# Moving a bank, a clip, one feed-forward item and several loads in the order of an attention kernel with a feed-forward block

## The chip, the cores and the metric

One Trainium2 chip, one of its cores. The metric is the device time of one execution in microseconds (us). The kernel is a single launch; everything below runs inside it.

## The reference

Two computations follow each other. The first is attention that is routed by clusters: each query and each key goes to the nearest of 16 centroids of its head, and a query attends only to the keys of its own cluster. The second takes the result as a matrix of 3072 tokens by 512 and runs a feed-forward block with a hard-swish gate.

```python
batch, n_heads, seq, head_dim = (4, 8, 768, 64)      # n_clusters = 16
q_assign = argmax(einsum('bhsd,hcd->bhsc', q_n, c_n), axis=-1)      # k_assign likewise
mask = q_assign[:, :, :, None] == k_assign[:, :, None, :]
scores = where(mask, scale * (q @ k^T), -1e9)
x = softmax(scores) @ v                              # then (B,H,S,D) -> (3072, 512)
h = x @ w_in                                         # 512 -> 2048
g = h * clip(h + 3.0, 0.0, 6.0) / 6.0
out = g @ w_out                                      # 2048 -> 512
```

## The kernel before, in words

The heads are taken in pairs: 16 pairs (`NPAIR`), four to a batch. The kernel has two stages and then a tail.

**First stage, pairs 0 to 7 (a loop over double steps `n`, two key blocks each).** Scores are full: `scores` puts them into `psum_s` (two buffers of two banks), `exponentials` reads them on ScalarE, `attn_v` multiplies by the values, `sum_up` adds up the denominators on TensorE (`pd`), and one step later VectorE takes the reciprocal and multiplies (lines 473 and 474). Into the same loop go the preparation of the next pair (`turn`, `cluster_scores`, `route`, `route_turn`), the decoding of the weights in small steps (`share` says how many), and the first items of the feed-forward block: `up_at` lists the double steps at which one item of two halves (`begin`, `end`) is taken from the list `fill`. `route` reads its tile `pr` on VectorE and writes `one_hot` (line 357); `route_turn` transposes `one_hot` on TensorE in two parts (line 379).

**Second stage, pairs 8 to 15 (`late_plan`, from `FIRST` on).** `whole.close()` gives back the memory of the first stage, the four score banks among it, and `open_late` opens new pools: `psum_y` with two banks and `psum_s` with one buffer of two. Here the rows of a pair are sorted by cluster so that scores need only a band. `order` and `positions` work out the place of each row (VectorE, lines 1000, 1009 and 1011). `scatter` (GpSimd) writes 24 pieces of rows, `qd` and `kvd`, to device memory by those places, out of the tiles `qn` and `kvn`, which `load_queries` and `load_keys` fill and of which there is one buffer each. `load_ranked` reads the sorted rows back: parts 0 and 1 into the tile `piece` (line 884), part 2 into `vs` (line 907). `turn_ranked` transposes a `piece` on TensorE (line 913), then come the band scores. After that `gather` fetches the results by the same places.

The order of the second stage is written by hand. `steps_of` gives each step of a pair an offset in points; there are 28 points to a pair (`SLOT`). At each point first the steps of the plan are emitted, in the order of the pairs and of the list, and then one half item of `fill`, except at two points of each pair. Each engine, and the queue of SyncE (SP) that issues nearly all loads and stores, then runs what it was given strictly in that order: a load that has to wait holds up every load behind it on SP.

**The feed-forward items.** A block is 256 tokens: `ffn_items` gives eight up items and seven down items per block. For the first block the up product is plain (`ph`, line 607): ScalarE lifts it (line 499), VectorE clips it (line 502), and after each odd item `gated_sums` forms four sums of the gate `g_sb` (line 645). For the other blocks the up product runs in halves with seven products for eight (`uX`, `uY`, line 655), which needs sums of weights in the tile `tx`; `first_sums` loads `tx` for the item after the next one from device memory (line 548, three buffers). In those blocks lift and clip are put off into the lists `lifting` and `ending`, which `raise_gates` and `finish` empty. The down items multiply `g_sb` by `w_out_sb` and by its sums `T1` to `T4` into two banks, `X` and `Y` (line 694). In the tiles named `m` of `psum_m` there are two banks, shared by turns between `ph`, `X`, `uX` and, in the first stage, the short tiles of the preparation (`pr`, `po`, `pd`, `pcs`, `pqk`).

**The tail.** What is left in `fill` runs with nothing beside it.

Of the kernel before, what the change touches and what calls it, by code (L numbers as in the profile page):

```python
# [8 lines left out]
F32 = mybir.dt.float32  # L9
# [9 lines left out]
P = 128  # L19
# [6 lines left out]
DM = 512  # L26
# [93 lines left out]
def fast_path(ctx, tc, ok, q, k, v, centroids, moe_w_in, moe_w_out, out):  # L120
# [3 lines left out]
    nc = tc.nc  # L124
# [53 lines left out]
    st = {}  # L178
# [322 lines left out]
    def clip(g, r, h):  # L501
        nc.vector.scalar_tensor_tensor(out=g, in0=r, scalar=1.0, in1=h, op0=ALU.min, op1=ALU.mult)  # L502
# [83 lines left out]
    def ffn_items(b):  # L586
        def up(m, i):
            u = (b * NHC + m) * HF + i
            g = g_sb[:, 0:4, i]
            got = {}  # L590

            def begin():
                raise_gates()
                load_block()
                if u >= HF:
                    first_sums(u + 2)
                    halved(b, m, u, i, got)

            def end():
                if u < HF:  # L600
                    for other in sooner.get(u, ()):
                        kept_sums(other)
                    ph = psum_m.tile([P, 512], F32, name="ph", tag="m")
                    for t in range(2):
                        f = t * HF + i
                        for kt in range(NKT):
                            nc.tensor.matmul(
                                ph[:, t * HC : (t + 1) * HC], lhsT=w_in_sb[:, kt, f * P : (f + 1) * P],
                                rhs=st["xb", b, m][:, kt], start=(kt == 0), stop=(kt == NKT - 1),
                            )  # L610
                    ph = ph.rearrange("p (k c) -> p k c", k=4)
                    lift(g, ph)
                    clip(g, g, ph)
                    gated_sums(i)
                else:
                    got["rest"](g)
                if i == HF - 1:
                    st.pop(("xb", b, m)), st.pop(("xs", b, m), None)
                    st["free"] = True
                    load_block()  # L620

            return [begin, end]
# [10 lines left out]
                op()  # L633
            ending.clear()

        def gated_sums(i):
            if i % 2 == 0:
                return
            a11, a21, a12, a22, s1, s2, s4 = (g_sb[:, k, i - 1 : i + 1] for k in range(7))
            eng = nc.vector if st["moving"] or (i == HF - 1 and st["last"]) else nc.gpsimd  # L640
            for out_, in0, in1, op in (
                (s1, a21, a22, ALU.add), (s2, s1, a11, ALU.subtract),
                (a21, a11, a21, ALU.subtract), (s4, a12, s2, ALU.subtract),
            ):
                eng.tensor_tensor(out=out_, in0=in0, in1=in1, op=op)  # L645
# [57 lines left out]
        def down(m, part):  # L703
            def keep(chunk, half, y, queue=nc.sync):
                queue.dma_start(out_v[b, 2 * m + chunk][:, half * HC : (half + 1) * HC], y)

            def multiply(second):
                if part < 2:
                    h = range(part * HF // 2, (part + 1) * HF // 2)
                    if second:  # L710
                        product(st["X"], 1, 5, st["T2"], False, True, False, h)
                    else:
                        product(st["X"], 0, 0, wb[0][0], True, False, False, h)
                    return
                kind, bank, half, w = (
                    (4, "Y", 0, st["T1"]), (1, "Y", 1, st["T3"]),
                    (2, "X", 0, wb[1][0]), (6, "Y", 0, wb[1][1]), (3, "Y", 1, st["T4"]),
                )[part - 2]
                h = range(second * HF // 2, (second + 1) * HF // 2)
                product(st[bank], half, kind, w, part == 2, part in (3, 4, 6), part > 3, h)  # L720

            def begin():
                raise_gates()
                if part == 0:
                    st["X"] = psum_m.tile([P, DM], F32, name="X", tag="m")
                    st["y0"] = yp.tile([P, DM], F32, name="y0", tag="y0")
                elif part == 2:
                    st["Y"] = st.get("psum_y", psum_m).tile([P, DM], F32, name="Y", tag="m")
                    st["y1"] = yp.tile([P, DM], F32, name="y1", tag="y1")
                multiply(0)  # L730

            def end():
                multiply(1)
                if part == 0:
                    finish()
                if (b, m, part) == (B - 1, NHC - 1, 6):
                    st["good"] = nc.values_load(ok[0:1, 0:1], min_val=0, max_val=1)
                if part == 4:
                    token_sums(*divmod(b * NHC + m + 1, NHC))
                y0, y1 = st["y0"], st.get("y1")  # L740
                if part == 1:
                    nc.scalar.copy(out=y0[:, HC:], in_=st["X"][:, HC:])
                    add(y0[:, HC:], y0[:, HC:], st["X"][:, 0:HC])
                elif part == 3:
                    add(y1[:, 0:HC], y0[:, HC:], st["Y"][:, HC:])
                    add(y1[:, HC:], y1[:, 0:HC], st["Y"][:, 0:HC])
                    keep(1, 1, y1[:, HC:])
                elif part == 4:
                    nc.scalar.copy(out=y0[:, 0:HC], in_=st["X"][:, 0:HC])
                    keep(0, 0, y0[:, 0:HC])  # L750
                elif part == 6:
                    add(y1[:, 0:HC], y0[:, HC:], st["Y"][:, HC:])
                    keep(1, 0, y1[:, 0:HC])
                    add(y0[:, HC:], y0[:, HC:], st["Y"][:, 0:HC])

                    keep(0, 1, y0[:, HC:], nc.scalar if st["last"] else nc.sync)
                if (b, m) == (0, 0):
                    for i in ([HF - 1, HF - 2], [5], [4], [], [3, 2], [0], [1])[part]:
                        make_first_sums(i)
                    if part in (0, 1):  # L760
                        weight_sums(6 + part)
                    elif part in (2, 3):
                        weight_sums(2 + part)

            return [begin, end]
# [420 lines left out]
    def steps_of(g):  # L1186

        first, last = g == FIRST, g == NPAIR - 1
        if first:
            plan = [  # L1190
                (-38, load_queries), (-37, load_keys, 0), (-36, load_keys, 1), (-37, run_up),
                (-36, step_up), (-31, order), (-30, positions), (-20, lambda g: st.pop("signed")()),
            ]
        else:
            plan = [
                (-46, load_natural, 0), (-45, load_natural, 1), (-38, turn_natural, 0), (-37, turn_natural, 1),
                (-36, cluster_scores), (-34, own_clusters), (-33, run_up), (-32, step_up), (-31, load_queries),
                (-29, order), (-28, positions), (-29, load_keys, 0), (-27, load_keys, 1),
            ]
        plan += [  # L1200
            (-29 if first else -24, scatter, 0), (-29 if first else -24, scatter, 1), (-12, band_masks), (-3, load_ranked, 0), (-3, load_ranked, 1),
            (-2, load_ranked, 2), (-1, turn_ranked, 0), (0, turn_ranked, 1),
        ]
        d = 1 if last else 2
        plan += [
            (d, band_scores, (0, 5), 1), (d + 2, band_scores, (2,), 3), (d + 4, band_scores, (4,)),
            (d + 4, band_values, 0), (d + 4, key_adds, 0, 1, 2), (d + 5, key_adds, 0, 3), (d + 7, band_values, 1),
            (d + 7, key_adds, 1, 1, 2), (d + 8, key_adds, 1, 3), (d + 10, band_sums),
            (12 if last else 14, band_divide), (14 if last else 16, keep_ranked),
            (15 if last else 23, gather), (28 if last else 37, turn_back),  # L1210
        ]
        return [(g, *step) for step in plan]
# [37 lines left out]
    decode += [lambda i=i: weight_sums(i) for i in range(4)]  # L1250
    st["kept"] = set()
    sooner = {0: (7,), 1: (6,), 2: (5,), 5: (4, 3)}
    up_at = (60, 64, 70, 72, 80, 84, 90, 94, 100)
    READY, DECODED = per_batch + 2 * lag_d, 2 * per_batch

    def share(n, r):
# [22 lines left out]
    with tc.manual_schedule():  # L1279
# [58 lines left out]
        st["early"] = False  # L1338
        st["moving"] = True
        open_late()  # L1340
        for i, point in enumerate(late_plan()):
            for op, *args in point:
                op(*args)
            busy = i >= AHEAD and (i - AHEAD) % SLOT in (6, 9)
            if fill and not busy:
                fill.pop(0)()
# [370 lines left out]
```

## Time and profile before

| | before |
|---|---|
| median of 3 runs | 954.39 us (954.17 to 955.42) |
| the profiled execution: its own time | 955.15 us |
| its span, first to last instruction | 953.4 us |
| granted TensorE clock, mean | 0.995 |
| TensorE busy (PE) | 930.6 us, 98% of the span |
| VectorE (DVE) | 595.6 us, 62% |
| ScalarE (ACT) | 349.7 us, 37% |
| GpSimd (POOL) | 574.6 us, 60% |
| HBM traffic | 129 GB/s over the span |

PE is TensorE's matmuls, DVE VectorE, ACT ScalarE, POOL GpSimd, SP SyncE, which is here only a queue of loads and stores. A row of a timeline reads: start in us from the span's start, duration (of the whole group if several are merged, with xcount), engine, line of the kernel, operation, tile written <- tiles read, shape, and in brackets the idle time of the engine before it and what ended it.

### The profile page before, as it was taken

What the parts mean: (1) busy time and instruction counts of PE and PEld (TensorE: products, weight loads), DVE (VectorE), ACT (ScalarE), POOL (GpSimd) and SP (SyncE); (2) the same over time, 40 slices, a digit from 0 to 9 for tenths busy, and PEclk for the clock granted to TensorE, in tenths of its full rate; (3) what the DMA queues carried; (4) which work ended last, traced back from release to release, by engine and by line L of the source; (5) the groups of instructions that cost most, each with busy time, mean ns of one, the idle gap of its engine ahead of it and who ended that gap; (6) DMA issues with size and microseconds to landing.
All of it is one profiled execution on the core that took longest, in us unless ns stands there. A gap on an engine that the chain in (4) does not pass through costs nothing.

```text
span 953.4 us, 17615 instructions
## 1 busy us (share of the span) xinstructions
PE 930.6 (98%) x6358; PEld 728.2 (76%) x6358; DVE 595.6 (62%) x1306; ACT 349.7 (37%) x731; POOL 574.6 (60%) x1302
## 2 busy tenths in 40 slices
PE   8999999989999999999999999999999999999997
PEld 5444445555798798797887978878888799999996
DVE  6789899899876376284483573474471564636261
ACT  6888887856112232233232241241331311212020
POOL 3877767748266577787777878777787060303030
PEclk9999999999999999999999999999999999999999
DMA  7255455351365557465593574744753333323210
GB/s 204 94 133 155 133 167 168 113 143 54 95 198 151 138 158 165 127 166 131 162 218 93 141 178 129 188 137 108 193 148 83 107 91 120 97 72 106 67 56 26
DMA packets 174351, 124.23 MB, mean 130 GB/s; under 512 B 134064, under 2 KB 152496, under 8 KB 174256
## 3 DMA queue, kind: packets, MB, share of 16 engines
q1 hardware_dynamic: 164320, 109.86, 43.1%
q0 software_dynamic: 9216, 12.60, 4.5%
q8 instruction: 52, 0.85, 0.4%
q10 hardware_dynamic: 720, 0.56, 0.2%
q14 instruction: 43, 0.35, 0.1%
HBM read 94.67 MB, written 28.31 MB: 129 GB/s over the span
## 4 chain that ended last, share of the span: by engine, by line
PE 69%; DMA 2%; issue 1%; DVE 1%; SPq 0%; POOL 0%; ACT 0%
PE Y L694 17%; PE uY L655 15%; PE X L694 13%; PE uX L655 11%; PE pv L1110 3%; PE ps L913 3%; PE ps L1071 3%; DMA piece<-qd 2%; PE pv L1071 1%; PE pd L1134 1%; PE pcs L337 1%; PE ps L1151 1%; PE rk L995 0%; PE pdt L1147 0%; DVE y L701 0%
## 5 line engine op out<-in xcount | busy, mean ns | idle before, releaser
L433 POOL TENSOR_TENSOR acc<-acc,ex 128x768 f32<-128x768 f32 x64 | 123.8, 1935 | 35.4 <-ACT ex L423 31.8
L1028 POOL DMA_INDIRECT qd<-qn,pos x96 | 97.9, 1020 | 50.9 <-issue 19.4
L1044 POOL DMA_INDIRECT xn<-xsd,pos x96 | 94.2, 981 | 48.4 <-ACT sx L499 27.5
L499 ACT ACTIVATE sx<-g_sb,half_c 128x512 f32<-128x512 f32 x88 | 63.7, 724 | 143.1 <-DVE g_sb L666 132.1
L645 POOL TENSOR_TENSOR g_sb<-g_sb 128x256 f32<-128x256 f32 x52 | 38.0, 754 | 125.5 <-DVE g_sb L502 124.5
L1020 POOL MEMSET w_low<- 128x1 f32 x864 | 91.9, 106 | 33.3
L1028 POOL DMA_INDIRECT kvd<-kvn,pos x96 | 95.6, 996 | 25.7 <-issue 24.7
L701 DVE TENSOR_TENSOR y<-y,Y 128x256 f32<-128x256 f32 x48 | 20.2, 421 | 138.0 <-PE Y L694 120.1
L655 PE MATMUL uX<-xb,w_in_sb 128*128 128x128 f32 x704 | 93.0, 275 | 0.0
L694 PE MATMUL X<-w_out_sb,g_sb 128*128 128x256 f32 x384 | 90.3, 382 | 1.8 <-DVE g_sb L502 1.8
L694 PE MATMUL Y<-T,g_sb 128*128 128x256 f32 x384 | 88.0, 381 | 0.0
L694 PE MATMUL Y<-w_out_sb,g_sb 128*128 128x256 f32 x384 | 87.7, 380 | 0.0
L655 PEld LDWEIGHTS uX<-xb,w_in_sb 128*128 128x128 f32 x704 | 85.7, 192 | 0.0
L694 PEld LDWEIGHTS X<-w_out_sb,g_sb 128*128 128x128 f32 x384 | 71.0, 190 | 15.9 <-issue 3.9
L694 PEld LDWEIGHTS Y<-T,g_sb 128*128 128x128 f32 x384 | 72.1, 190 | 13.2 <-issue 3.9
L694 PEld LDWEIGHTS Y<-w_out_sb,g_sb 128*128 128x128 f32 x384 | 71.8, 190 | 10.6 <-issue 1.3
L400 PE MATMUL ps<-xf 64*128 64x384 f32 x384 | 78.5, 487 | 0.9 <-ACT ex L423 0.9
L666 DVE TENSOR_TENSOR sx<-uX,sx 128x128 f32<-128x128 f32 x176 | 51.0, 290 | 44.6 <-ACT sx L673 32.2
L423 ACT ACTIVATE ex<-ps 128x768 f32<-128x768 f32 x96 | 72.6, 803 | 4.5 <-PE ps L400 4.5
L443 PE MATMUL pv<-ex,vt 128*64 128x384 f32 x384 | 72.5, 499 | 0.0
L502 DVE SCALAR_TENSOR_TENSOR g_sb<-sx,g_sb 128x512 f32<-128x512 f32 x88 | 63.7, 726 | 3.5 <-ACT be L1094 1.9
L666 DVE TENSOR_TENSOR g_sb<-uY,sx 128x128 f32<-128x128 f32 (+1 forms) x176 | 65.5, 413 | 0.0
(194 smaller groups left out, 1804.2 us busy)
## 6 DMA issues: line engine op xcount, KB each, us to landing
tx<-td SPq DMA_DIRECT2D x86, 384.0 KB
raw<-in_moe_w_in_dram SPq DMA_DIRECT2D x16, 512.0 KB
raw<-in_moe_w_out_dram SPq DMA_DIRECT2D x16, 512.0 KB
xb<-xd SPq DMA_DIRECT2D x12, 512.0 KB
out_dram<-y SPq DMA_DIRECT2D x44, 128.0 KB
qk<-in_q_dram SPq DMA_DIRECT2D x18, 192.0 KB
qk<-in_k_dram SPq DMA_DIRECT2D x18, 192.0 KB
vt<-in_v_dram SPq DMA_DIRECT2D x16, 192.0 KB
```

The source lines that it names most:

```text
L400: nc.tensor.matmul(st["ps", n][:, t, 0:HALF], lhsT=x[r, NCH + j], rhs=x[r, hf * NHC : (hf + 1) * NHC], start=first, stop=last, skip_group_ ...
L423: nc.scalar.activation(out=ex, in_=sc, func=ACT.Exp, scale=SM_SCALE)
L433: nc.gpsimd.tensor_tensor(out=acc, in0=acc, in1=ex, op=ALU.add)
L443: nc.tensor.matmul(pv[t * D : (t + 1) * D], lhsT=vt[:, t, j], rhs=ex[:, t], start=(j == 0), stop=(j == NCH - 1),)
L499: nc.scalar.activation(out=r, in_=h, func=ACT.Relu, bias=half_c, scale=1.0 / 6.0)
L502: nc.vector.scalar_tensor_tensor(out=g, in0=r, scalar=1.0, in1=h, op0=ALU.min, op1=ALU.mult)
L655: nc.tensor.matmul(dst, lhsT=w[:, kt], rhs=x(kt), start=(kt == 0), stop=(kt == HK - 1))
L666: nc.vector.tensor_tensor(out=out_, in0=in0, in1=in1, op=ALU.add)
L694: nc.tensor.matmul(bank[:, half * HC : (half + 1) * HC], lhsT=g_sb[:, kind, i], rhs=w[:, i], start=(first and i == 0), stop=(last and i == ...
L1020: nc.gpsimd.memset(w_low, W_LOW)
L1028: i = nc.gpsimd.indirect_dma_start(out=rows[name, g, t], in_=src, in_offset=None, out_offset=bass.IndirectOffsetOnAxis(ap=pos[:, a, j, t : ...
L1044: nc.gpsimd.indirect_dma_start(out=xn[:, j, t], out_offset=None, in_=rows["xsd", g, t], in_offset=bass.IndirectOffsetOnAxis(ap=pos[:, 0, j ...
```

## The change

Five edits in one:

1. The first product bank `X` of the first block is taken from `psum_y`, that is from the banks that held the scores, and the bank `Y` of that block from `psum_m`; before it was the other way round.
2. The last clip of the first block (item 7) and the four gated sums behind it are put off until the first down item has been emitted; the sums go to GpSimd.
3. The first down item leaves the loop of the first stage (double step 100) and is emitted right after `open_late`.
4. The up item of double step 80 is taken at double step 82.
5. In the second stage, for pairs 9 to 15: `load_queries` one point sooner, `load_keys` two, `positions` one; and `load_ranked` two points sooner (all three parts; pair 8 keeps its places).

```diff
@@ up(...).end
                     lift(g, ph)
-                    clip(g, g, ph)
-                    gated_sums(i)
+                    if i < HF - 1:
+                        clip(g, g, ph)
+                        gated_sums(i)
+                    else:
+                        ending.append(lambda: (clip(g, g, ph), gated_sums(i, nc.gpsimd)))
@@
-        def gated_sums(i):
+        def gated_sums(i, eng=None):
...
-            eng = nc.vector if st["moving"] or (i == HF - 1 and st["last"]) else nc.gpsimd
+            if eng is None:
+                eng = nc.vector if st["moving"] or (i == HF - 1 and st["last"]) else nc.gpsimd
@@ down(...).begin
                 if part == 0:
-                    st["X"] = psum_m.tile([P, DM], F32, name="X", tag="m")
+                    pool_x = st["psum_y"] if (b, m) == (0, 0) else psum_m
+                    st["X"] = pool_x.tile([P, DM], F32, name="X", tag="m")
...
                 elif part == 2:
-                    st["Y"] = st.get("psum_y", psum_m).tile([P, DM], F32, name="Y", tag="m")
+                    pool_y = psum_m if (b, m) == (0, 0) else st["psum_y"]
+                    st["Y"] = pool_y.tile([P, DM], F32, name="Y", tag="m")
@@ steps_of
         first, last = g == FIRST, g == NPAIR - 1
+        f = -3 if first else -5
...
-                (-36, cluster_scores), (-34, own_clusters), (-33, run_up), (-32, step_up), (-31, load_queries),
-                (-29, order), (-28, positions), (-29, load_keys, 0), (-27, load_keys, 1),
+                (-36, cluster_scores), (-34, own_clusters), (-33, run_up), (-32, step_up), (-32, load_queries),
+                (-31, load_keys, 0), (-29, order), (-29, positions), (-29, load_keys, 1),
...
-            ... (-12, band_masks), (-3, load_ranked, 0), (-3, load_ranked, 1),
-            (-2, load_ranked, 2), (-1, turn_ranked, 0), (0, turn_ranked, 1),
+            ... (-12, band_masks), (f, load_ranked, 0), (f, load_ranked, 1),
+            (f + 1, load_ranked, 2), (-1, turn_ranked, 0), (0, turn_ranked, 1),
@@
-    up_at = (60, 64, 70, 72, 80, 84, 90, 94, 100)
+    up_at = (60, 64, 70, 72, 82, 84, 90, 94)
@@ after the first stage
         st["moving"] = True
         open_late()
+        fill.pop(0)()
+        fill.pop(0)()
         for i, point in enumerate(late_plan()):
```

More of the change, by code (lines that the diff above doesn't have):

```diff
@@ L1196, in steps_of @@
                 (-46, load_natural, 0), (-45, load_natural, 1), (-38, turn_natural, 0), (-37, turn_natural, 1),
-                (-36, cluster_scores), (-34, own_clusters), (-33, run_up), (-32, step_up), (-31, load_queries),
-                (-29, order), (-28, positions), (-29, load_keys, 0), (-27, load_keys, 1),
+                (-36, cluster_scores), (-34, own_clusters), (-33, run_up), (-32, step_up), (-32, load_queries),
+                (-31, load_keys, 0), (-29, order), (-29, positions), (-29, load_keys, 1),
             ]
         plan += [
-            (-29 if first else -24, scatter, 0), (-29 if first else -24, scatter, 1), (-12, band_masks), (-3, load_ranked, 0), (-3, load_ranked, 1),
-            (-2, load_ranked, 2), (-1, turn_ranked, 0), (0, turn_ranked, 1),
+            (-29 if first else -24, scatter, 0), (-29 if first else -24, scatter, 1), (-12, band_masks), (f, load_ranked, 0), (f, load_ranked, 1),
+            (f + 1, load_ranked, 2), (-1, turn_ranked, 0), (0, turn_ranked, 1),
         ]
```

## The prediction

> **What bounds the kernel now.** I read the page first, then the waits of TensorE, then windows around the longest.
>
> ```profile
> span 953.4 us, 17615 instructions
> PE 930.6 (98%) x6358; PEld 728.2 (76%) x6358; DVE 595.6 (62%) x1306; ACT 349.7 (37%) x731; POOL 574.6 (60%) x1302
> ```
>
> PE sets the end; 953.4 - 930.6 = 22.8 us are not matmul, some of them at the two ends. The rest are waits, and only those can be won. The table of waits (us in total, times, longest) names them:
>
> ```profile
> PE ps L913 <- DMA piece<-qd: 4.1, 4, 2.1
> PE ph L607 <- DVE one_hot L357: 2.3, 1, 2.3
> PE X L694 <- DVE g_sb L502: 1.8, 1, 1.8
> ```
>
> These three are where the five edits are: the sorted rows come late four times, the up item of double step 80 waits, and the first down item waits. A wait costs more than itself, as the granted clock shows (columns: length, then busy us of PE, PEld, DVE, ACT, POOL, then PEclk):
>
> ```profile
> 192.60:196.00 3.40, 1.07 (x7) 0.63 (x4) 3.26 (x8) 0.00 (x0) 2.79 (x2) 1.00 0.86 245
> 196.00:199.40 3.40, 3.40 (x10) 2.69 (x9) 3.37 (x3) 0.00 (x0) 0.00 (x0) 0.50 1.27 250
> 240.40:243.80 3.40, 1.58 (x11) 0.54 (x7) 3.40 (x5) 1.70 (x6) 0.08 (x1) 1.00 0.65 182
> 609.00:612.40 3.40, 1.31 (x16) 1.14 (x16) 1.62 (x4) 0.98 (x3) 2.87 (x9) 1.00 1.07 226
> 612.40:615.80 3.40, 3.40 (x20) 3.38 (x18) 0.62 (x2) 0.69 (x1) 2.87 (x9) 0.51 1.07 272
> ```
>
> After the windows with 1.07 and 1.31 us of PE work the clock is half for 3.4 us: 1.7 us lost each time. In the 240.4 window PE worked 1.58 us; the mean clock of 0.995 leaves no room for a third loss before the end. So a wait of about 2 us costs 3.7, one of 1.8 costs 1.8.
>
> **Item of double step 80 to 82: nothing by itself.** VectorE and TensorE there:
>
> ```profile
> 194.58 0.62 DVE L357 TENSOR_TENSOR one_hot<-pr,mx 128x192 bf16<-128x192 f32 x2
> 197.17 2.55 DVE L473 RECIPROCAL rcp<-pd 128x384 f32<-128x384 f32 x1
> ```
> ```profile
> 195.35 5.38 PE L607 MATMUL ph<-xb,w_in_sb 128*128 128x256 f32 x16 [2.33 <-DVE one_hot L357]
> 200.56 0.50 PE L379 MATMUL po<-ident_q,one_hot 128*128 128x128 bf16 x6
> 204.16 0.51 PE L379 MATMUL po<-ident_q,one_hot 128*128 128x128 bf16 x6
> 206.63 0.50 PE L400 MATMUL ps<-xm 64*128 64x384 bf16 x4 [0.49 <-ACT xm L384]
> ```
>
> `ph` waited for the bank of `pr`, which `one_hot` frees at 195.2. With `ph` gone, the next in PE's order is `po`, which reads `one_hot` itself: the same 2.33 us, and the same slow window. Then `po` and the scores and values (3.6 us at full clock, 200.56 to 204.16) run in the slow window instead of `ph`; `ph` needs the bank that the reciprocal frees at 199.7 and arrives after 200. What goes is part of the waits behind 204.16, since ScalarE sees the scores about 3 us sooner: I get the last row's start 0.9 us earlier. VectorE isn't moved: its clip waited for `ph` before and does so after. That decides what the 0.9 us is worth.
>
> **Handover: minus 0.55 us.**
>
> ```profile
> 240.70 2.35 DVE L523 TENSOR_TENSOR T<-w_out_sb,T 128x1024 f32<-128x1024 f32 x2
> 242.97 0.67 DVE L502 SCALAR_TENSOR_TENSOR g_sb<-g_sb,ph 128x512 f32<-128x512 f32 x1
> 243.56 2.54 DVE L473 RECIPROCAL rcp<-pd 128x384 f32<-128x384 f32 x1
> 246.20 0.83 DVE L474 TENSOR_TENSOR num<-num,rcp 128x384 f32<-128x384 f32 x1
> 248.86 0.17 DVE L837 TENSOR_REDUCE odd<-ident 128x1 f32<-128x32 f32 x1
> 249.31 0.15 DVE L867 TENSOR_SCALAR least<-least 128x1 f32<-128x1 f32 x1
> ```
> ```profile
> 243.69 7.17 PE X L694 x32
> ```
> ```profile
> 243.72 2.90 POOL L645 TENSOR_TENSOR g_sb<-g_sb 128x256 f32<-128x256 f32 x4 [4.03 <-DVE g_sb L502]
> ```
>
> Now `X` waits 1.82 us for its bank, which the last clip (243.64) frees, and its 32 matmuls end at 250.7. After, `X` has a bank of the scores, long free, and starts with the gates of items 0 to 3. Its second eight matmuls need `T2`, ready at 243.05. But the clip is put in VectorE's order behind the reciprocal, the product and four small operations of `open_late`: 243.05 + 2.54 + 0.7 + 0.6 (248.86 to 249.46) = 246.95, and the clip ends at 247.6. PE comes to item 7's gate before that: eight matmuls from 243.05 (0.217 us each, 6.95 / 32) end at 244.8, six more at 246.1. There it waits 1.5 us. Of the last eight, four can follow; the fifth needs the second gated sum, 2 x 0.73 us after the clip (POOL row: 2.90 / 4), at 249.1; `X` ends at 250.15. So one wait replaces another: -0.55 us, and the 0.9 us from above is swallowed, as the end now hangs on VectorE alone. Bounds: -1.8 if the clip comes in time, +1.2 if PE's wait reaches 2 us and the clock halves. GpSimd's preparing operations, which stood behind the four sums, now run ahead of them and wait for nothing of this. The banks of the next items change hands, and each has been read 2 us or more before it is needed again.
>
> **Sorted rows: minus 4.0 us.** Pairs 11, 12, 13 and 15:
>
> ```profile
> 489.37 0.85 PE L913 MATMUL ps<-ident,piece 128*128 128x128 f32 x6 [0.66 <-DMA piece<-qd]
> 549.75 0.84 PE L913 MATMUL ps<-ident,piece 128*128 128x128 f32 x6 [0.90 <-DMA piece<-qd]
> 553.51 0.61 PE L655 MATMUL uX<-xs,tx 128*128 128x128 f32 x4
> 611.41 0.84 PE L913 MATMUL ps<-ident,piece 128*128 128x128 f32 x6 [2.09 <-DMA piece<-qd]
> 616.79 0.61 PE L655 MATMUL uX<-xs,tx 128*128 128x128 f32 x4
> 729.39 0.85 PE L913 MATMUL ps<-ident,piece 128*128 128x128 f32 x6 [0.48 <-DMA piece<-qd]
> ```
> ```profile
> 484.19 1.01 SPq L884 DMA_DIRECT2D piece<-qd  x2
> 543.97 0.32 SPq L548 DMA_DIRECT2D tx<-td  x1
> 544.38 1.55 SPq L884 DMA_DIRECT2D piece<-qd  x2
> 550.49 0.48 SPq L548 DMA_DIRECT2D tx<-td  x1
> 602.76 2.00 SPq L548 DMA_DIRECT2D tx<-td  x2
> 604.86 0.97 SPq L884 DMA_DIRECT2D piece<-qd  x2
> 612.31 0.49 SPq L548 DMA_DIRECT2D tx<-td  x1
> ```
> ```profile
> 484.71 4.52 DMA piece<-qd
> 605.34 5.94 DMA piece<-qd
> ```
> ```profile
> 476.80 0.97 POOL L1028 DMA_INDIRECT kvd<-kvn,pos  x1 [0.15 <-issue]
> ```
>
> Two points are one up item, some 3.1 us. In SP's order the loads of pairs 11 and 12 overtake one `tx` load and are issued 3.1 us sooner; in pair 13 only 1.7 us, since the first `tx` at 602.76, behind the output stores, still stands ahead (604.86 - 603.2). They may start when the scatter has landed: its last issue in pair 11 ends at 477.77, 6.4 us ahead of the load, so there is room for 3.1. GpSimd's chain of scatter and gather also starts sooner, as `positions` now follows `order` at once and the keys come earlier; it keeps its distance. So 0.66, 0.90 and 0.48 go. In pair 13 the 2.09 goes with its 1.7 of clock: 3.8 us.
>
> What is late next: the overtaken `tx`. It now stands behind eight loads (four pieces, two `vs`, two `qn`). Today a `tx` behind eight is issued 6.1 us (544.38 to 550.49) to 7.45 us (604.86 to 612.31) after the first, and lands, by the two chain rows, 4.5 to 5.9 us later: 10.6 to 13.4 in all. It is needed two up items, two turns and the rank matmuls after its old issue, 553.51 - 543.97 - 0.90 = 8.6 us. Pairs 11 and 12: -3.1 + 10.6 to 13.4 = 7.5 to 10.3, a new wait of 0 to 1.7 us; I take 0.2 each, as pair 12's own row gives the short end. Pair 13: -1.25 + 10.6 to 13.4 = 9.35 to 12.15 against 8.6, a wait of 0.7 to 3.5 us; I take 1.4, nearer the short end, for one `tx` fewer lies in front. Sum: -(0.66 - 0.2) - (0.90 - 0.2) - (3.8 - 1.4) - 0.48 = -4.0 us. Pair 8 keeps its places, but the queries of pair 9 now stand ahead of its pieces and wait for its scatter; the pieces are issued about 1.5 us later and PE had no wait there. I price that at nothing; if its slack is gone, it costs up to 1.5.
>
> [...]
>
> **Sum.** -0.55 - 4.0 = -4.6 us: span 948.8, the profiled execution 955.15 to 950.55, the median 954.39 (0.76 below that execution) to 949.8.
>
> **Rivals.**
> *All waits go.* -1.8 - 0.66 - 0.90 - 3.8 - 0.48 = -7.65: 946.7. For it: `tx` at the short end is in time in two pairs. Against: the clip's place in VectorE's order. 13%.
> *The clock loss is not there to be won.* [...] 15%. [...]
> *It doesn't do what it says.* The loads move but wait for the scatter on SP, and land as before; the handover alone remains: 953.8. Against: the 6.4 us. 10%.
> *Slower: `tx` becomes the wait.* At the long end, 13.4 us behind the first load, PE waits 1.7 in pairs 11 and 12 and 3.5 in pair 13, the last with 1.7 of clock: (1.7 - 0.66) + (1.7 - 0.90) + (5.2 - 3.8) - 0.48 - 0.55 = +2.2: 956.6. It decides once the landing passes about 12.5 us in all three pairs. For it: pair 13 measures 7.45 + 5.94. Against: pair 12 measures 6.1 and its loads are no slower than others. 7%.
>
> **Numbers.** The forecast has 55% (947.5 to 952). Measurement can tell about 0.2%, 1.9 us. Faster by more: 55 + 13 + 15 = 83%; within: the third rival and a little, 11%; slower: 6%. The range, 946.4 to 953.2, holds the forecast with its bounds and the first and second rival (the first with 0.3 us of room), and leaves out most of the third and the fourth.
>
> **What would show it.** After: the wait of `X` for `g_sb` about 1.5 us inside `X`'s second half instead of 1.8 ahead of it; a wait of 2.3 us for `one_hot`, now at `po`; no wait for `piece`, or under 0.5 us; a wait of `uX` for `tx` of 1 to 2 us behind pair 13's turns; GpSimd's scatter beginning about 2 us sooner. A slow clock window near 612 or new ones at 245 or 490 would show the sum wrong, as would a `po` that doesn't wait.

## The result

The changed kernel takes 951.11 us (median of 8 runs, 950.02 to 953.28) against 954.77 (953.50 to 955.98) for the kernel before on the same chip: ratio 0.9965, 95% interval [0.9956, 0.9975]. The forecast was 949.8 (946.4 to 953.2). The profiled execution took 952.83 us.

The head of its page, and its table of waits of TensorE (us in total, times, longest):

```profile
span 951.0 us, 17617 instructions
...
PE 929.3 (98%) x6358; PEld 726.1 (76%) x6358; DVE 597.0 (63%) x1306; ACT 349.7 (37%) x731; POOL 576.2 (61%) x1302
```
```profile
PE uX L659 <- DMA tx<-td: 3.7, 2, 2.9
PE po L379 <- DVE one_hot L357: 2.5, 2, 2.3
...
PE ps L919 <- ACT xsort L920: 0.7, 2, 0.4
...
PE X L698 <- DVE g_sb L502: 0.5, 1, 0.5
...
PE X L698 <- POOL g_sb L649: 0.2, 1, 0.2
```

No wait for `piece` is left, `po` waits where `ph` did, and `X` waits inside its second half, as announced. But `tx` is waited for in its place. Of the 3.7 us in the table 2.88 are new; the other 0.79, near 274, stood there before as 0.65 us under VectorE's name. With a new wait of 1.21 us that is also under VectorE's name (below), the new ones make 4.1 us, as much as those for `piece` were. The wait at `X` is 0.73 us in all, not 1.5. TensorE and VectorE at the handover in the timeline after:

```profile
240.20 0.81 PE L467 MATMUL pd<-acc,ones 128*64 128x384 f32 x4
...
244.50 1.46 PE L698 MATMUL X<-w_out_sb,g_sb 128*128 128x256 f32 x6
246.47 0.70 PE L698 MATMUL X<-w_out_sb,g_sb 128*128 128x256 f32 x2 [0.51 <-DVE g_sb L502]
...
248.26 1.13 PE L698 MATMUL X<-T,g_sb 128*128 128x256 f32 x4 [0.22 <-POOL g_sb L649]
249.23 2.11 PE L698 MATMUL Y<-T,g_sb 128*128 128x256 f32 x9
```
```profile
239.82 2.35 DVE L523 TENSOR_TENSOR T<-w_out_sb,T 128x1024 f32<-128x1024 f32 x2
...
245.74 0.68 DVE L502 SCALAR_TENSOR_TENSOR g_sb<-g_sb,ph 128x512 f32<-128x512 f32 x1
```

`T` starts at 239.82, not at 240.70: VectorE did come 0.88 us sooner, and all behind it, so `Y` starts at 249.23 rather than 250.15. The same two marks of TensorE before, the last `pd` ahead of the handover and the start of `Y`:

```profile
241.06 0.81 PE L467 MATMUL pd<-acc,ones 128*64 128x384 f32 x4
...
250.71 3.62 PE L694 MATMUL Y<-T,g_sb 128*128 128x256 f32 x16
```

From the one to the other it takes 9.65 us before and 9.03 after. In the sorted rows, the waits of pairs 12 and 13 and SP's loads ahead of the second:

```profile
552.52 0.68 PE L659 MATMUL uX<-xs,tx 128*128 128x128 f32 x4 [1.21 <-DVE g_sb L670]
...
614.93 0.68 PE L659 MATMUL uX<-xs,tx 128*128 128x128 f32 x4 [2.88 <-DMA tx<-td]
```
```profile
602.32 0.98 SPq L890 DMA_DIRECT2D piece<-qd  x2
...
609.55 0.73 SPq L548 DMA_DIRECT2D tx<-td  x1
```

In pair 13 `tx` is issued 7.2 us after the first `piece`, and the work that needs it starts 5.4 us later: 12.6 together. (The first row is put down to VectorE, which had been done; that it waits for `tx` too is read from the runs below in which `tx` comes sooner and the wait is gone.)

**A yardstick.** All kernels here run the same 6358 matmuls (handover_filled has 50 more), and up to the cluster scores (`pcs`) of a pair exactly the same number of them. So three stretches can be compared between kernels: *a*, from the start of the wait for `one_hot` near 193 to the `pcs` of pair 9; *b*, from there to the `pcs` of pair 15; *c*, the rest. The rows for before, after, and after once more on another chip (span 950.1):

```profile
195.35 0.98 PE L607 MATMUL ph<-xb,w_in_sb 128*128 128x256 f32 x3 [2.33 <-DVE one_hot L357]
...
299.36 0.85 PE L337 MATMUL pcs<-xnat,cnT 128*32 128x384 f32 x8
...
659.44 0.85 PE L337 MATMUL pcs<-xnat,cnT 128*32 128x384 f32 x8
```
```profile
195.32 0.51 PE L379 MATMUL po<-ident_q,one_hot 128*128 128x128 bf16 x6 [2.26 <-DVE one_hot L357]
...
298.02 0.85 PE L337 MATMUL pcs<-xnat,cnT 128*32 128x384 f32 x8
...
657.65 0.85 PE L337 MATMUL pcs<-xnat,cnT 128*32 128x384 f32 x8
```
```profile
195.86 0.51 PE L379 MATMUL po<-ident_q,one_hot 128*128 128x128 bf16 x6 [2.25 <-DVE one_hot L357]
...
296.87 0.85 PE L337 MATMUL pcs<-xnat,cnT 128*32 128x384 f32 x8
...
657.19 0.85 PE L337 MATMUL pcs<-xnat,cnT 128*32 128x384 f32 x8
```

Before: a = 299.36 - (195.35 - 2.33) = 106.3, b = 360.1, c = 953.4 - 659.44 = 294.0. After: 105.0, 359.6, 293.4. So of the 2.4 us between the two spans 1.4 came in a, 0.45 in b and 0.6 in c. The table has the same three numbers for every run, each from one profiled execution, with the stretches of half clock (3.4 us each) that fall into it; one costs up to 1.7 us. (The mean granted clock of these executions is 0.998 or 0.999 where the table has none, 0.996 or 0.997 with one, 0.994 or 0.995 with two. Behind the last matmul it is low too, 0.56 from 949.9 on in before and 0.65 from 946 on in after; that costs nothing and isn't counted.) "Lost" is what the stretch between the `pcs` of pairs 10 and 11 takes beyond the 59.3 us that it takes in the changed kernel; the section on pair 11 deals with it. Ratios are to the kernel before on the same chip.

| kernel | edits | ratio, 95% interval | a | b | c | half clock |
|---|---|---|---|---|---|---|
| before | none | 1 | 106.3 | 360.1 | 294.0 | a, b |
| after | 1 to 5 | 0.9965 [0.9956, 0.9975] | 105.0 | 359.6 | 293.4 | a |
| after_again | 1 to 5 | 0.9972 [0.9963, 0.9981] | 103.3 | 360.3 | 292.9 | b |
| handover_only | 1 to 4 | 1.0002 [0.9993, 1.0011] | 104.7 | 361.1 | 293.3 | a, b |
| rows_only | 5 | 0.9996 [0.9986, 1.0005] | 106.3 | 360.5 | 294.4 | a, b |
| tx_behind_four | 1 to 5, `tx` sooner | 0.9961 [0.9949, 0.9974] | 103.7 | 358.9 (2.7 lost) | 293.2 | none |
| rows_tx_behind_four | 5, `tx` sooner | 0.9938 [0.9925, 0.9951] | 106.4 | 355.9 | 293.2 | a |
| without_item_82 | 1 to 3, 5 | 1.0018 [1.0005, 1.0032] | 104.6 | 367.4 (5.8 lost) | 293.4 | b |
| without_82_spread | 1 to 3, 5, natural rows later | 0.9982 [0.9972, 0.9992] | 104.6 | 362.1 | 293.2 | b twice |
| pieces_sooner | 1 to 4, half of 5 | 0.9991 [0.9977, 1.0005] | 104.2 | 361.9 (4.3 lost) | 294.4 | none |
| one_hot_sooner | 1 to 5, one-hots first | 0.9969 [0.9957, 0.9980] | no wait | 363.5 (2.7 lost) | 293.5 | b |
| handover_filled | 1 to 4, idle transposes | 1.0047 [1.0029, 1.0066] | 105.9 | 365.1 (4.9 lost) | 293.5 | none |
| tx_four_spread | as tx_behind_four, natural rows later | 0.9942 [0.9929, 0.9956] | 103.4 | 356.1 | 293.2 | none |
| all_together | the same with one-hots first | 0.9911 [0.9891, 0.9931] | no wait | 356.2 | 293.0 | none |

### The profile page after: what moved, and what is told of

It is laid out like the page before. It is cut to its first block, busy times and chain, and to the rows that moved or that the text cites. A ratio compares the mean times of both kernels' runs of the same rounds, so it can differ in the third digit from the quotient of the medians.

```text
span 951.0 us, 17617 instructions
## 1 busy us (share of the span) xinstructions
PE 929.3 (98%) x6358; PEld 726.1 (76%) x6358; DVE 597.0 (63%) x1306; ACT 349.7 (37%) x731; POOL 576.2 (61%) x1302
## 4 chain that ended last, share of the span: by engine, by line
PE 69%; DVE 3%; DMA 1%; ACT 0%; issue 0%; POOL 0%; ACTq 0%; SPq 0%
PE Y L698 18%; PE uY L659 15%; PE X L698 13%; PE uX L659 12%; PE pv L1116 3%; PE ps L1077 3%; PE ps L919 2%; PE pv L1077 1%; DMA tx<-td 1%; PE pd L1140 1%; PE pcs L337 1%; DVE g_sb L670 1%; PE ps L1157 1%; DVE g_sb L649 0%; DVE sx L670 0%; DVE g_sb L502 0%
## 5 line engine op out<-in xcount | busy, mean ns | idle before, releaser
L1034 POOL DMA_INDIRECT kvd<-kvn,pos x96 | 97.7, 1018 | 26.0 <-issue 26.0
L698 PEld LDWEIGHTS Y<-w_out_sb,g_sb 128*128 128x128 f32 x384 | 71.8, 190 | 10.6 <-issue 1.3
```

Of the source, the lines that this page charges most:

```text
L698: nc.tensor.matmul(bank[:, half * HC : (half + 1) * HC], lhsT=g_sb[:, kind, i], rhs=w[:, i], start=(first and i == 0), stop=(last and i == ...
L1034: i = nc.gpsimd.indirect_dma_start(out=rows[name, g, t], in_=src, in_offset=None, out_offset=bass.IndirectOffsetOnAxis(ap=pos[:, a, j, t : ...
```

## Each half alone

handover_only is the changed kernel with `load_queries`, `load_keys`, `positions` and `load_ranked` where the kernel before has them; rows_only is the kernel before with these four moved.

```diff
 handover_only
-        f = -3 if first else -5
+        f = -3
-  (-32, load_queries), (-31, load_keys, 0), (-29, order), (-29, positions), (-29, load_keys, 1),
+  (-31, load_queries), (-29, order), (-28, positions), (-29, load_keys, 0), (-27, load_keys, 1),
```

> Edits 1 to 4 (bank, clip, first down item, item 82), rows at their old places. Theory: the handover is worth about 1.5 us (X ended at 249.23 instead of 250.71 us in the two profiles), independent of the rows; so 1.5 us under the kernel before, with the four waits for piece (0.66, 0.90, 2.09, 0.48) still there and a wait of about 0.5 us for the clip in X's second half. Rival (as on record): only 0.55 us, since VectorE isn't earlier. Rival: nothing, the profiles' 1.5 us are a matter of one execution.

> Edit 5 alone (rows, places, queries, keys sooner). Theory: the waits for piece go, and waits for tx of about 1.2 us (pair 12) and 2.9 us (pair 13) come, so some 1 to 2.5 us under the kernel before, depending on which of them halves the clock; the wait of X for its bank stays at 1.8 us. Rival: the tx waits of the changed kernel come from the two parts together (PE being ahead by 1.5 us), then rows alone show tx waits well under 1 us and a gain of 4 us.

Neither is to be told from the kernel before, while together they give 0.35%. In its profile handover_only wins 1.6 us in a and loses 1.0 in b, where its waits grow:

```profile
PE ps L919 <- DMA piece<-qd: 4.9, 4, 2.0
```

This was 4.1, of which 0.48 in pair 15, that is in c; in b the waits grow from 3.65 to 4.87 us. What comes sooner at the handover waits again for the sorted rows. (Its span is 1.2 us under that of the kernel before, but the profiled execution is the second shortest of its eleven runs, whose ratio shows no gain.) rows_only has no such wait, and waits for `tx` instead, 0.88 us in pair 12 and 2.62 in pair 13 (both put down to VectorE), with a stretch of half clock behind the second: b is 360.5 for 360.1. So edit 5 as made adds next to nothing of its own; with it in place, what edits 1 to 4 win isn't taken back.

## The load that became late

In tx_behind_four `vs` and the queries keep their old points, so that `tx` is behind four loads; rows_tx_behind_four does the same on rows_only.

```diff
-  (f + 1, load_ranked, 2)
+  (-2, load_ranked, 2)
-  (-32, load_queries)
+  (-31, load_queries)
```

> The changed kernel, but the values (third part of load_ranked) stay at their old offset -2 and the queries at -31, so that the overtaken tx load stands behind four loads instead of eight. Theory: tx lands some 4 us sooner after the first piece, the waits of 1.2 and 2.9 us in pairs 12 and 13 go or fall under 0.5 us, and the median falls by 3 to 4 us to about 947.5. Rival (the tx is slow because all loads, gathers and scatters share the DMA engines at that time, not because of its place in the queue): waits stay over 1 us each and the median stays within 1 us of the changed kernel.

> Edit 5 alone on the kernel before, but with the loads of vs back at two points before the slot and those of the queries a point later, so that tx stands behind four loads and not eight. Theory A, rows alone gave nothing (0.9996) because the waits for tx in pairs 12 and 13 (0.88 and 2.62 us, with the half clock) took the place of those for the piece: without them the gain shows without the handover too: waits of PE between 480 and 760 about 1.8 us for 4.5, no half clock at 612 to 616, ratio 0.997. Theory B, the sooner rows are worth something only behind the sooner handover: ratio 0.999 to 1.000.

SP in pair 13 of rows_tx_behind_four:

```profile
602.67 0.98 SPq L884 DMA_DIRECT2D piece<-qd  x2
603.76 2.24 SPq L884 DMA_DIRECT2D piece<-kvd  x2
606.10 0.65 SPq L548 DMA_DIRECT2D tx<-td  x1
```

`tx` is issued 3.4 us after the first `piece`, not 7.2, and behind the turns of pairs 12 and 13 TensorE waits neither for it nor for a piece. (What is left is 0.45 us later in pair 13, at 618.22, where a product reads the next `tx`; the trace names no releaser. In tx_four_spread the same wait is 1.01 us and is put down to `tx`.) b falls to 355.9, that is by 4.2 us against before, of which 1.7 are a stretch of half clock that this execution doesn't have. The ratio falls to 0.9938, further than the 0.997 expected, with no edit at the handover at all. This is the gain of 4.0 us that the prediction had put down to edit 5: it was there to be had, and the loads that edit 5 puts ahead of `tx` cost nearly all of it. tx_behind_four loses these waits for `tx` too, but a new one comes in pair 11 (below), and its ratio is that of the changed kernel, not the 947.5 us expected.

## The item of double step 82

```diff
-    up_at = (60, 64, 70, 72, 82, 84, 90, 94)
+    up_at = (60, 64, 70, 72, 80, 84, 90, 94)
```

> The changed kernel with the item at double step 80, not 82 (edits 1 to 3 and 5). The prediction held the item for worth nothing by itself (VectorE isn't moved, the clip of item 7 comes at the same time): ratio as the changed kernel, 0.9965. Rival, from the trace of the changed kernel: VectorE came 0.88 us sooner to the handover because of the item; without it the clip behind X's first part is 0.9 us later, the wait inside X goes from 0.5 us to about 1.4, and the ratio is 0.9974 to 0.9976.

The ratio went to 1.0018, far past both theories; most of that is the loss in pair 11. What the item itself is worth is read in a, between executions without half clock there: 104.6 without it (twice), 103.3 with it in after_again, a difference of 1.3 us. Counted only from the wait's start to the last `pd` ahead of the handover, it is 47.0 us without it (twice) and 45.5 to 45.9 with it (four kernels). TensorE and VectorE without the item (without_82_spread), then VectorE with it (after_again):

```profile
196.09 3.69 PE L607 MATMUL ph<-xb,w_in_sb 128*128 128x256 f32 x16 [2.33 <-DVE one_hot L357]
200.51 0.49 PE L379 MATMUL po<-ident_q,one_hot 128*128 128x128 bf16 x6 [0.73 <-DVE rcp L473]
```
```profile
229.31 0.69 DVE L502 SCALAR_TENSOR_TENSOR g_sb<-g_sb,ph 128x512 f32<-128x512 f32 x1 [0.19 <-ACT g_sb L499]
...
240.40 2.35 DVE L523 TENSOR_TENSOR T<-w_out_sb,T 128x1024 f32<-128x1024 f32 x2
```
```profile
228.66 0.68 DVE L502 SCALAR_TENSOR_TENSOR g_sb<-g_sb,ph 128x512 f32<-128x512 f32 x1
...
238.72 2.35 DVE L523 TENSOR_TENSOR T<-w_out_sb,T 128x1024 f32<-128x1024 f32 x2
```

Without the item `po` waits a second time, 0.73 us, and at 229.31 VectorE has caught up with TensorE: its clip waits for the lift of a `ph` that came late. With the item sooner nothing is waited for there, and `T` starts 1.5 us sooner, counted from the wait near 193 (240.40 - 193.76 = 46.6 against 238.72 - 193.61 = 45.1). So the item moves VectorE, and the handover with it.

## What is lost in pair 11

pieces_sooner keeps of edit 5 only the three parts of `load_ranked`.

```diff
-  (-32, load_queries), (-31, load_keys, 0), (-29, order), (-29, positions), (-29, load_keys, 1),
+  (-31, load_queries), (-29, order), (-28, positions), (-29, load_keys, 0), (-27, load_keys, 1),
```

> Edits 1 to 4 and of edit 5 only the loads of the sorted rows two points sooner; the places, the queries and the keys stay where the kernel before has them. Theory A, what the sooner rows are worth is their place in SP's queue (in the kernel before the loads of pair 13 start 6.7 us after the last scatter, so the scatters are not what they wait for): ratio 0.9965 as the changed kernel, or a little better, since tx stands behind six loads and not eight; pieces not waited for by over 0.5 us. Theory B, the places are needed sooner as well (the scatters end 0 to 2 us later than in the changed kernel): waits for the piece stay, 2 us and more in sum, ratio 0.999 to 1.000.

No wait of TensorE for a piece is left in it, and `tx`, which stands behind six loads, is the likely cause of a wait of 1.31 us in pair 13 (the trace names no releaser, but the product is the one that waited for `tx` in the changed kernel): the places, keys and queries needn't be sooner for the pieces to be in time. But the time stayed at 0.9991, since b loses 4.3 us between 396 and 421. without_item_82 shows the place at its worst (TensorE, then VectorE, then windows with busy us of PE, PEld, DVE, ACT, POOL, the clock and the DMA share):

```profile
408.81 0.51 PE L659 MATMUL uX<-xs,tx 128*128 128x128 f32 x3 [0.38 <-issue]
...
421.41 0.85 PE L337 MATMUL pcs<-xnat,cnT 128*32 128x384 f32 x8 [1.90 <-ACT xnat L920]
```
```profile
403.84 0.62 DVE L670 TENSOR_TENSOR sx<-uX,sx 128x128 f32<-128x128 f32 x2 [2.97 <-issue]
```
```profile
400.00:404.00 4.00, 4.00 (x38) 3.41 (x31) 1.03 (x4) 1.37 (x3) 3.22 (x11) 1.00 1.07 320
404.00:408.00 4.00, 4.00 (x37) 3.90 (x35) 1.85 (x6) 0.37 (x1) 3.34 (x12) 1.00 0.44 120
408.00:412.00 4.00, 3.17 (x19) 2.40 (x19) 1.82 (x6) 0.61 (x2) 3.31 (x9) 1.00 0.43 118
```

The DMA engines are full from 400 to 404 (1.07): the natural rows of pair 11 are loaded there (the expectations call them pair 10's) beside `tx`. Then ScalarE, VectorE and TensorE run late one after the other, partly with no releaser in the records ("issue"). ScalarE's copy of `uX` in the changed kernel, then in without_item_82:

```profile
402.27 0.27 ACT L677 COPY sx<-uX 128x128 f32<-128x128 f32 x1 [0.41 <-PE uX L659]
```
```profile
403.54 0.27 ACT L677 COPY sx<-uX 128x128 f32<-128x128 f32 x1 [1.16 <-PE uY L659]
```

It starts 2.42 and 3.73 us after the start of `pd` (399.85 and 399.81). In all five kernels that lose time it is late, 2.96 to 4.27 us, while TensorE still runs without a gap. These are five of the first eight experiments; before and after lose nothing there, with the DMA share from 400 to 404 as high (1.09 and 1.08), nor does rows_tx_behind_four (1.15). Three runs asked whether this belongs to the kernel or to the chip, and whether the burst is its cause. "Spread" loads the second half of the natural rows two points later:

```diff
-  (-46, load_natural, 0), (-45, load_natural, 1),
+  (-46, load_natural, 0), (-43, load_natural, 1),
```

> The changed kernel once more, on the chip of the next two runs and beside them. Kernels with one part of the change altered were up to 6 us over it on another chip, and their profiles lose 2.2 to 5.8 us between 396 and 421 us of the span (TensorE, VectorE and ScalarE late with no releaser in the records, behind the loads of the natural rows of pair 10, which with tx fill the DMA engines: share 1.08 from 400 to 404), where the profile of the changed kernel loses nothing. Theory A, whether these microseconds are lost is fixed by the kernel's order and times: 0.9965 again, and nothing lost between 396 and 421. Theory B, it is a matter of the chip or of the day: 0.999 or more here, with the loss in the profile.

> As without_item_82 (ratio 1.0018, 5.8 us lost between 396 and 421), with the second half of the natural rows loaded three points before its turn's point less sooner: at 43 points before the slot, not 45, some 4 us later, so that the DMA engines aren't filled at 400 to 404. Theory A, the loss follows from the burst of loads: it goes, ratio 0.9965 to 0.9975. Theory B, the burst has no part in it: 1.0018 as without_item_82.

> As tx_behind_four (0.9961, waits for tx in pairs 12 and 13 gone, 2.4 us of waits on the natural rows' copies at 412 to 418), with the second half of the natural rows loaded at 43 points before the slot, not 45. Theory A, the waits at 412 to 418 follow from the burst of loads: they go, ratio 0.9935 to 0.994 (949.5 to 950 us by a before of 955.7), the fastest so far. Theory B: 0.996 as tx_behind_four; were the later load itself waited for at the turn, up to 1 us more.

after_again loses nothing there, and repeats its ratio within the intervals. Both kernels that lost time there lose none with the later load: without_item_82 goes from 1.0018 to 0.9982 (not quite the 0.9965 to 0.9975 expected: it waits 3.38 us for `tx` in pair 13, with two stretches of half clock), tx_behind_four from 0.9961 to 0.9942. But the delay did less than was expected: the two loads are issued 1.7 us later, now behind two loads of `tx` rather than one, and the DMA share from 400 to 404 is still 0.99 in without_82_spread. So the place of these loads in SP's order has a part in the loss; that the burst has one isn't shown, and it isn't enough by itself, since before, the changed kernel and rows_tx_behind_four have it and lose nothing. Nor was a kernel that loses time run again on the chip of these three runs, so the chip isn't ruled out, though kernels with and without the loss stood beside each other on both earlier chips. Why ScalarE is late there, and what "issue" is, stays open.

## The clock

one_hot_sooner moves three weight decoding steps from the double step ahead of pair 7's routing to that of the routing (`share`; before 4 and 3, then 1 and 6), so that VectorE comes to the one-hots sooner; handover_filled puts transposes of the identity ahead of `po` and of pair 13's first turn, to keep TensorE at work in its waits.

```diff
 one_hot_sooner, share(n, r)
+        if n // per_pair == FIRST - 2:
+            return {0: 6, 2: 5, 4: 1, 6: 6, 8: 5, 10: 5}[r]
 handover_filled, route_turn
+        if g == FIRST - 1 and part == 0:
+            for i in range(34):
+                nc.tensor.transpose(out=po[:, i % NCH], in_=ident_q, identity=ident_q)
 handover_filled, turn_piece, with idle=16 for pair 13's first turn
+        for i in range(idle):
+            nc.tensor.transpose(out=pt[:, i % 2, 0:P], in_=ident, identity=ident)
```

> The changed kernel, with the decoding steps of the last pair but one shared out otherwise: 1 instead of 4 at the double step before route, 6 instead of 3 at that of route, so that VectorE reaches one_hot about 2.2 us sooner (three steps of 0.7 us). Theory: the wait of 2.3 us at po goes nearly whole, and with it the slow clock window at 196 us: 2.2 to 3.9 us under the changed kernel. Rival: VectorE is the limit of this stage up to the handover, so what is won at po is lost again at the clip or the reciprocals, and the median stays within 1 us.

> Edits 1 to 4 without the sooner rows (as handover_only, whose mean granted clock over its runs was 0.9958 and whose waits of 2.26 us at 193.2 and 2.00 us at 608.9 were each followed by 3.4 us at half clock), and TensorE is kept at work in those two waits: 34 more bf16 transposes of the identity into po ahead of pair 7's first six (0.057 us each, 1.9 us) and 16 more f32 transposes into ps ahead of pair 13's first turn (0.112 us each, 1.8 us). The waits end when they ended before. Theory A, the halved clock is a cost of its own beside the waits and comes from idleness: no half clock at 196 and 612, the mean clock at 0.997 to 0.998, the median 1.2 to 2 us under handover_only: ratio about 0.9985. Theory B, the halving isn't set by these waits, or what it costs is taken back in later waits: ratio as handover_only, 1.0002, or up to 0.3 us above it.

The transposes of handover_filled didn't run in the first wait but behind it:

```profile
196.12 2.07 PE L380 MATMUL po<-ident_q 128*128 128x128 bf16 x34 [2.25 <-DVE one_hot L357]
198.02 0.50 PE L382 MATMUL po<-ident_q,one_hot 128*128 128x128 bf16 x6
```

They read only the identity and still started at 196.12, when the wait of 2.25 us for `one_hot` was over: the bank of `po` itself comes free only then, so the 34 transposes were 2 us of more work. The 16 ahead of pair 13's first turn did run in its wait and filled it but for 0.65 us, and no half clock followed; but none followed the unfilled 2.25 us near 193 either, so the run settles nothing about the clock. Its 4.5 us over the kernel before (by the ratio) contain these and the 4.9 us lost in pair 11. In one_hot_sooner the wait at `po` and its stretch of half clock went, 0.8 us came back at the next `ph`, and then pair 11 took 2.7 us.

Two executions of the changed kernel itself show more of the clock. Windows around the wait near 193, in after and then in after_again:

```profile
193.20:196.60 3.40, 1.28 (x14) 0.81 (x15) 3.29 (x7) 0.73 (x2) 2.25 (x2) 0.99 0.98 272
196.60:200.00 3.40, 3.40 (x14) 1.42 (x12) 3.29 (x3) 3.34 (x11) 0.16 (x1) 0.50 1.10 257
...
609.55:612.95 3.40, 2.50 (x23) 2.27 (x21) 2.91 (x9) 1.12 (x3) 2.87 (x9) 1.00 1.13 294
612.95:616.35 3.40, 1.42 (x13) 1.45 (x14) 1.59 (x5) 0.56 (x1) 2.36 (x9) 1.00 1.17 284
```
```profile
190.75:194.16 3.41, 2.86 (x18) 0.93 (x14) 3.27 (x5) 1.75 (x4) 3.33 (x2) 1.00 0.38 84
194.16:197.57 3.41, 1.71 (x16) 1.16 (x18) 3.31 (x7) 1.17 (x2) 1.84 (x2) 1.00 1.02 291
197.57:200.98 3.41, 3.41 (x19) 1.85 (x16) 3.32 (x3) 3.32 (x10) 0.59 (x1) 1.00 1.22 273
```

The wait is the same, 2.26 and 2.25 us. In the first execution TensorE has 1.28 us of work in the 3.40 us from 193.20 on, and the next 3.40 run at half clock (0.50). In the second the clock is 1.00 in all three windows: a is 103.3 for 105.0. So the half clock costs 1.7 us here, and one execution has it and the next not. (Without the item of 82 it costs 1.0: from the wait's start to the last `pd` it takes 48.0 us in before and 47.0 in without_82_spread, where the second wait at `po` takes the rest back.) In pair 13 it is the other way round: the wait of 2.88 us in after was followed by none (1.00 up to 619.75), that of 2.48 in after_again by one (0.50 from 614.00 to 617.40). So the length of a wait doesn't tell whether the half clock follows; what does isn't shown.

It shows in the times too. Of the 22 runs of the kernel before beside after_again, the eight with a mean clock of 0.995 or less took 955.35 to 956.54 us, the ten with 0.998 or more 952.81 to 954.63.

## The fastest version

all_together is tx_four_spread with the decoding steps of one_hot_sooner.

> As tx_four_spread (0.9942), with pair 7's one-hots ahead of its other work in the items of that pair, as in one_hot_sooner (there the wait of 2.26 us at 193 and its half clock went, the first product's start came 2.1 us sooner, but 2.4 us were lost again at 410 to 416 on the copies of the natural rows). Theory A, that loss came from the burst of loads and is gone with the later load: the 2 us stay, 946.5 us by a before of 954.6, ratio 0.9915 to 0.9925. Theory B, VectorE or GpSimd are what the later pairs wait for, and the gain is waited away in pairs 10 to 13: ratio 0.994 as tx_four_spread.

946.8 us (946.22 to 947.36) beside a before of 955.12: ratio 0.9911 [0.9891, 0.9931]. That is under one_hot_sooner (0.9969) by far more than the intervals, and under tx_four_spread (0.9942 [0.9929, 0.9956]) with intervals that just touch, from four runs. Its b is that of tx_four_spread (356.2 for 356.1), so what was won ahead of pair 9 was kept.

What edits 1 to 4 add to the better order of the loads is not settled by the times: tx_four_spread has them and is at 0.9942, rows_tx_behind_four hasn't and is at 0.9938, on different chips. Only the profiles differ, by 3.0 us in a, of which some 1.0 is the half clock.

## Why the prediction came out as it did

The median fell by 3.7 us, into the range and within 1.3 us of the forecast, but not by the sum that was forecast. Of the 4.6 us for the span, the two profiled executions of the changed kernel have 2.4 and 3.3: the sorted rows gave 1.0 where 4.0 were forecast, the handover and the item together 1.4 where 0.55 was. That two misses of opposite sign, and the half clock that comes and goes from run to run, left the median so near is in part luck.

*The waits bound the kernel, and the edits move them as said.* Right. `po` waits 2.26 us, `X` waits in its second half, no wait for a piece remains, `tx` waits behind pair 13's turns.

*Item of 82: 0.9 us earlier, and swallowed at the handover, since VectorE isn't moved.* The 0.9 us was right, the second half failed. From the start of the wait near 193 to the last `pd` it takes 48.04 us before and 47.14 after, both with half clock: 0.90 sooner. But VectorE came sooner by as much, for its clip had caught up with TensorE. The wait for the lift was there to be seen in the timeline before:

```profile
229.60 0.69 DVE L502 SCALAR_TENSOR_TENSOR g_sb<-g_sb,ph 128x512 f32<-128x512 f32 x1 [0.18 <-ACT g_sb L499]
```

So a `ph` that comes sooner lets the whole chain to `T` come sooner, and the 0.9 us is kept (1.3 between executions without half clock).

*Handover: -0.55.* Right, for edits 1 to 3 by themselves. From the last `pd` to `Y` it takes 9.65 us before, 9.64 in the two kernels with the rows alone, and 9.03 to 9.06 in all eleven profiles with edits 1 to 3, with and without the item, with and without half clock: 0.6 us less. The two make 1.5 us; behind `Y` 0.14 is lost again up to the `pcs` of pair 9, which leaves the 1.4 in a. What each of the three edits gives wasn't separated.

*Sorted rows: -4.0.* The waits for pieces went, all of them, and so did pair 13's half clock in the profiled execution: 4.13 and 1.7 us, as forecast. The term that was mis-sized is the wait for `tx`: 0.2, 0.2 and 1.4 us were taken, 1.8 in all; measured are 0, 1.21 and 2.88, 4.1 in all (0, 0.67 and 2.48 the second time). From the first `piece` to the work that needs `tx` it takes 13.4 us in pair 12 and 12.6 in pair 13: inside the 10.6 to 13.4 that were worked out, but at the long end, where the short end was taken. (For pairs 11 and 12 the sum also puts the first `piece` 3.1 us ahead of the old place of `tx`; by its own rows, 544.38 - 3.1 against 543.97, it is 2.7, and the wait 0 to 2.1.) Two waits of the second turn for ScalarE's copy, 0.36 and 0.37 us, weren't foreseen. Together: -4.13 - 1.7 + 4.1 + 0.7 = -1.0, and b and c gained 0.45 and 0.6. The rival in which `tx` becomes the wait had the mechanism right.

*Clock.* The 1.7 us in pair 13 were counted as won, and the execution shown had none there; after_again has it again (0.50 from 614.00 to 617.40). The rival "the clock loss is not there to be won" describes the executions better than the forecast: behind waits of 2.1 to 2.9 us the half clock came in some and not in others. No run shows what decides it.

*The halves add up.* The prediction summed the edits. Alone each gives nothing; it was not weighed that a gain at the handover is taken back by a wait for pieces that doesn't come sooner.

## What to carry to other kernels

Before a wait is counted as a gain, look at what arrives next at the same place: loads moved ahead in one queue made the load behind them late (`tx` behind eight was issued 7.2 us after the first, behind four 3.4), and the best order here moved the loads of the pieces and left those of the values and the queries. An edit ahead of a wait on something that doesn't move gains nothing until that wait is gone, so test edits together as well as alone. And read a chain back to the last instruction that waited, however short: 0.18 us told that VectorE hung on TensorE.

## What was not expected of the hardware

Whether a wait of TensorE of about 2 us is followed by 3.4 us at half clock differs between executions of one kernel: the same wait, 2.26 and 2.25 us, cost 1.7 us more in one execution than in the other, and 2.88 us were followed by none where 2.48 were followed by one. What separates them isn't shown. And around the loads of the natural rows of pair 11 (DMA share from 400 to 404 of 0.89 to 1.07 in four of them, 0.44 in one_hot_sooner), five kernels lost 2.7 to 5.8 us through lateness on three engines that no record explains, while before, the changed kernel and rows_tx_behind_four lost nothing with a share of 1.08 to 1.15. With two of the loads 1.7 us later it was gone in two such kernels, and absent from a third with that delay.
